# Decode block with cached attention: weights moved behind the cache rows, late weights loaded last, values in 512-column products, the output projection gathered on GpSimd

## The chip, the cores and the metric

The kernel runs on one core of a Trainium2 chip. A core has TensorE (PE, matrix products into PSUM), VectorE (DVE), ScalarE (ACT), GpSimd (POOL), a sequencer that here only issues transfers (SP), and 16 DMA engines that move data between HBM and the on-chip SBUF, a memory of 128 partitions. The engines run side by side and meet at semaphores. The metric is the device time of one execution in microseconds (us), lower is better; it is given as the median of several runs.

## The reference

One token (batch 1, sequence 1) goes through a conditioned block: modulation from `c`, layer norm, attention with 32 heads over a cache of 8192 positions with head size 192, output projection, second layer norm, and a two-layer network with a squared ReLU. All of it is float32. Cut to what matters:

```python
mod = (_silu(c) @ w_mod).reshape(c.shape[0], 6, 1, -1)      # c: 640, w_mod: 640 x 3840
sa, ca, ga, sb, cb, gb = (mod[:, 0], ..., mod[:, 5])
h = _layernorm(x) * (1 + ca) + sa
q = (h @ wq).reshape(B, Sq, 32, 192).transpose(0, 2, 1, 3)   # wq: 640 x 6144
scores = einsum("bhqd,bhkd->bhqk", q, k_cache) * 192 ** -0.5 # k_cache: 32 x 8192 x 192
o = einsum("bhqk,bhkd->bhqd", softmax(scores), v_cache)
x = x + ga * (o.reshape(B, Sq, 6144) @ wo)                   # wo: 6144 x 640
h = _layernorm(x) * (1 + cb) + sb
x = x + gb * (relu(h @ w1 + b1) ** 2 @ w2 + b2)              # w1: 640 x 1536, w2: 1536 x 640
```

The key and value caches are 201.3 MB each; wq and wo are 15.7 MB each, w_mod is 9.8 MB, w1 and w2 are 3.9 MB each. Everything is read once.

## The kernel before, in words

**Layout.** The 8192 positions of a head lie 64 to a partition, so a head's keys are a tile of 128 x 64 x 192 numbers (49,152 bytes in each partition, 6.29 MB) and its values another. Three such tiles (`slot`, line 47) fit at a time; every big load takes the next of them in turn. A load can therefore be issued only when the tile three loads earlier has been read for the last time.

**Start.** SP issues `wm0` (the columns of w_mod for sa and ca), the first pair's wq, `wm1` (the columns for ga, sb and cb) and the first head's keys. `mod` (lines 121 to 129) multiplies the modulation weights by silu(c) on TensorE; `layernorm` gives h; `query` (lines 172 to 178) makes the query of a pair of heads, already copied to all partitions.

**Loop over heads** (lines 257 to 274). Each turn issues the loads of the head's keys and values and, once for each pair of heads, a load `w` of 1.97 MB with this pair's wo and the next pair's wq (`load_w`, tiles of their own). `keys` (lines 183 to 200) works on four chunks of 16 positions: DVE multiplies the chunk by the query in place (line 190) and sums 9 to 12 of the 16 rows (line 192), ACT sums the remaining 4 to 7 (line 195). Between the chunks stand `inverse` of the head before and, in turn, `project` of the pair before (even heads) or `query` of the next pair (odd heads). `softmax` (lines 208 to 220) takes the maximum over all positions with a TensorE product, and ACT writes the exponentials 16 times side by side. `values` (lines 222 to 230) multiplies them with the values in 32 products of 384 columns (two positions each), four at a time in the four column groups of TensorE. One fp32 product is two TensorE instructions, each with a weight load.

**Project** (lines 232 to 250) scales the two heads' outputs on DVE, turns them into columns on TensorE (line 241), copies them, and multiplies them with wo into the sum `att` that stands in PSUM over the whole loop.

**End.** SP issues w1 and then `gw_t`, which holds the last columns of w_mod (gb) ahead of w2. The last pair is projected; then come x1, the second layer norm, the products with w1 (line 299), the squared ReLU, gb (`mod`, line 307), the products with w2 (line 315) and the output.

The engines' order is the order in which the program is written (`manual_schedule`); each engine works through its own instructions in that order.

Of the kernel before, what the change touches and what calls it, by code (L numbers as in the profile page):

```python
# [13 lines left out]
P = 128  # L14
D = 640
# [12 lines left out]
I = 16  # L28
NCH = NPOS // I
N_ACT = (7, 6, 6, 4)  # L30
TAIL_PARTS = 4
WO = 3 * D
WQ = KB * PW
W2_CUT = ((0, 6), (6, 5), (11, 1))
# [4 lines left out]
def block_kernel(ctx: ExitStack, tc: tile.TileContext, xc, kc, vc, wq0, wx, wo15, wm0, wm1, w1, gw2, bb, out):  # L39
# [7 lines left out]
    def slot(name):  # L47
        return strm.tile([P, NPOS * DH], F32, tag="slot", name=name, bufs=3)


# [4 lines left out]

    pick = const.tile([P, 2, 32], F32, name="pick")
    nc.vector.memset(pick[:, 0], 0.0)
    nc.vector.memset(pick[:, 1], 1.0)
    for g in range(G):
        nc.vector.memset(pick[32 * g:32 * g + 16, 0], 1.0)  # L60
        nc.vector.memset(pick[32 * g:32 * g + 16, 1], 0.0)
# [49 lines left out]


# [4 lines left out]
    nc.vector.tensor_mul(e, e, c_c)  # L117

    mods = const.tile([P, 6, DG], F32, name="mods")

    def mod(first, n, w):

        ps = psum.tile([P, 512], F32, tag="q", name=f"ps_mod{first}", bufs=2)
        for b in range(KB):
            wb = w[:, b].rearrange("p (m n) -> p m n", m=n)
            for g in range(G):
                nc.tensor.matmul(ps[32 * g:32 * (g + 1), :n * DG], e[:, b:b + 1].to_broadcast([P, 32]),  # L127
                                 wb[:, :, DG * g:DG * (g + 1)], start=(b == 0), stop=(b == KB - 1))
        nc.vector.tensor_copy(mods[:, first:first + n], ps[:, :n * DG].rearrange("p (m n) -> p m n", m=n))  # L129

    wm0_t = slot("wm0_t")
    nc.sync.dma_start(wm0_t[:, :KB * 2 * D], wm0)

    qb_t, w_t = {}, {}

    def load_w(i):

        w_t[i] = strm.tile([P, WO + WQ], F32, tag="w", name=f"w{i}", bufs=2)
        if i < 0:
            nc.sync.dma_start(w_t[i][:, WO:], wq0)  # L140
        elif i + 1 == NPAIR:
            nc.sync.dma_start(w_t[i][:, :WO], wo15)
        else:
            nc.sync.dma_start(w_t[i], wx[i])

    k_t, v_t = {}, {}

    def load(src, to, h, what):
        to[h] = slot(f"{what}{h}")
        n = TAIL_PARTS if h == H - 1 and what == "v" else 1  # L150
        w = NPOS * DH // n
        for c in range(n):
            nc.sync.dma_start(to[h][:, c * w:(c + 1) * w],
                              src[h].rearrange("(p i) d -> p (i d)", p=P)[:, c * w:(c + 1) * w])

    load_w(-1)
    wm1_t = slot("wm1_t")
    nc.sync.dma_start(wm1_t[:, :KB * 3 * D], wm1)
    load(kc, k_t, 0, "k")
    mod(0, 2, wm0_t[:, :KB * 2 * D].rearrange("p (b n) -> p b n", b=KB))  # L160
    ma = columns(mods[:, 0:2].rearrange("p m n -> p (m n)"), 2 * DG, "ma")
# [10 lines left out]
    def query(i):  # L172
        w = w_t[i - 1][:, WO:].rearrange("p (b n) -> p b n", b=KB)
        ps = psum.tile([P, 512], F32, tag="q", name=f"ps_q{i}", bufs=2)
        for b in range(KB):
            nc.tensor.matmul(ps[:, :PW], hR[:, b], w[:, b], start=(b == 0), stop=(b == KB - 1))  # L176
        qb_t[i] = work.tile([P, PW], F32, name=f"qb{i}", tag="qb")
        nc.scalar.activation(qb_t[i], ps[:, :PW], AF.Copy, scale=DH ** -0.5)

    att = psum.tile([P, 512], F32, tag="att", name="att")  # L180
    query(0)

    def keys(h, between):
# [3 lines left out]
        t = k_t.pop(h).rearrange("p (i d) -> p i d", d=DH)  # L187
        for c in range(NCH):
            pr = t[:, c * I:(c + 1) * I]
            nc.vector.tensor_mul(pr, pr, q[:, None, :].to_broadcast([P, I, DH]))  # L190
            n = I - N_ACT[c]
            nc.vector.tensor_reduce(sc[:, c * I:c * I + n], pr[:, :n], axis=AX.X, op=ALU.add)  # L192
            for i in range(n, I):
                jk = work.tile([P, DH], F32, tag="jk", name=f"jk{h}_{c}_{i}", bufs=2)
                nc.scalar.activation(jk, pr[:, i], AF.Copy, accum_out=sc[:, c * I + i:c * I + i + 1])  # L195
            if c == 0 and h:
                inverse(h - 1)
            if c == 2:
                between()
        return sc  # L200

    ri_t, ps_t, sum_t = {}, {}, {}

    def inverse(h):
        ri_t[h] = work.tile([P, 1], F32, tag="ri", name=f"ri{h}", bufs=3)
        nc.vector.reciprocal(ri_t[h], sum_t.pop(h))

    def softmax(h, sc):
# [3 lines left out]
        nc.tensor.matmul(ps[:, :P], mp.to_broadcast([P, P]), ident, start=True, stop=True)  # L212
# [3 lines left out]
        p = work.tile([P, NPOS, 16], F32, tag="p", name=f"p{h}", bufs=1)  # L216
        sp = work.tile([P, 1], F32, tag="sp", name=f"sp{h}")
        nc.scalar.activation(p, sc[:, :, None].to_broadcast([P, NPOS, 16]), AF.Exp, bias=nm, accum_out=sp)  # L218
        sum_t[h] = total(sp, f"sum{h}")
        return p  # L220

    def values(h, p):

        t = v_t.pop(h)
        ps_t[h] = psum.tile([P, 512], F32, tag="o", name=f"ps_o{h}", bufs=3)
        n = NPOS // 2
        for j in range(n):
            g = j % G
            nc.tensor.matmul(ps_t[h][32 * g:32 * (g + 1), :PW], p[:, 2 * j:2 * j + 2].rearrange("p e r -> p (e r)"),  # L229
                             t[:, PW * j:PW * (j + 1)], start=(j < G), stop=(j >= n - G))  # L230

    def project(i):
        os_ = work.tile([P, 2, PW], F32, tag="os", name=f"os{i}", bufs=1)
        for a in range(2):
            h = 2 * i + a
            nc.vector.tensor_scalar(os_[:, :, DH * a:DH * (a + 1)], ps_t.pop(h)[:, :PW].rearrange("p (e d) -> p e d", e=2),  # L236
                                    ri_t.pop(h), None, op0=ALU.mult)
        pt = psum.tile([P, 512], F32, tag="sm", name=f"ps_oT{i}", bufs=2)
        for j in range(3):
            for k in range(2):  # L240
                nc.tensor.matmul(pt[:, 32 * j:32 * (j + 1)], os_[:, k, P * j:P * (j + 1)], pick[:, k],  # L241
                                 start=(k == 0), stop=(k == 1))
        oT = work.tile([P, 96], F32, tag="oT", name=f"oT{i}")
        nc.vector.tensor_copy(oT, pt[:, :96])  # L244
# [117 lines left out]
```

## Time and profile before

| What | Value |
|---|---|
| Median of 3 runs | 1074.64 us (1073.70 to 1075.82) |
| Profiled execution, first to last instruction | 1072.6 us |
| PE / DVE / ACT / POOL busy | 431.8 / 756.2 / 320.1 / 0.7 us |
| Instructions | 8839, of them 3176 products and 3176 weight loads on PE |
| HBM read | 451.82 MB |
| Mean DMA rate | 422 GB/s |

The profile is one execution. Its page gives the busy time of each engine, a strip of 40 slices with the DMA rate, the DMA queues, the chain of waits that ended last, and groups of instructions by source line with count, busy time and the mean of one in ns. Other views give one row for a stretch of time (busy time of each engine with the number of instructions in brackets, granted TensorE clock, DMA share, GB/s), single instructions in order of time, or who waited for whom. "SPq" is SP's sequencer, where transfers are issued.

### The profile page before, as it was taken

The page shows a single profiled execution, that of the slowest core. Times are in us where ns is not written, and L with a number is a line of the kernel's source. Part 1 is how long each engine was busy: PE and PEld are TensorE (multiplying, and loading weights), DVE is VectorE, ACT ScalarE, POOL GpSimd, SP SyncE. Part 2 cuts the span into 40 slices and gives each one's busy share as a digit, 9 for nine tenths or more (in the row PEclk, how much of TensorE's full clock was granted, in tenths as well). Part 3 has the DMA queues.
Part 4 walks back from the last instruction along what each step waited for, and adds up shares of the span by engine and source line. Part 5 has one row for each costly group of instructions (what it writes and reads, how often), then busy time and mean ns, then how long its engine had stood idle before and what let it go on. Part 6 is the DMA issues. An engine that isn't in the chain of part 4 may idle for free.

```text
span 1072.6 us, 8839 instructions
## 1 busy us (share of the span) xinstructions
PE 431.8 (40%) x3176; PEld 205.0 (19%) x3176; DVE 756.2 (70%) x453; ACT 320.1 (30%) x1559; POOL 0.7 (0%) x6
## 2 busy tenths in 40 slices
PE   3243243435425353442436344242633434363246
PEld 1011121113112121211113122111312111131113
DVE  1675877858578685858868586885757778585872
ACT  1132332323233232323422233332322323232340
POOL 0000000000000000000000000000000000000000
PEclk8666566666656666575666656566665666666568
DMA  9999999999999999999999999999999999999976
GB/s 401 438 426 435 419 442 436 428 431 433 428 422 442 424 439 424 437 429 427 435 437 424 440 424 438 425 432 432 426 436 423 430 435 426 433 428 426 399 292 266
DMA packets 13299, 452.38 MB, mean 422 GB/s; under 512 B 1732, under 2 KB 1736, under 8 KB 2120
## 3 DMA queue, kind: packets, MB, share of 16 engines
q1 hardware_dynamic: 12968, 451.81, 98.1%
q8 instruction: 25, 0.41, 0.2%
q14 instruction: 18, 0.15, 0.0%
q10 hardware_dynamic: 288, 0.01, 0.0%
HBM read 451.82 MB, written 0.00 MB: 421 GB/s over the span
## 4 chain that ended last, share of the span: by engine, by line
DMA 41%; DVE 38%; PE 18%; ACT 2%; issue 1%; SPq 0%; DVEq 0%; ACTq 0%
DMA k<-in_kc 41%; DVE k L190 21%; DVE sc L192 14%; PE ps_o L229 11%; PE ps_oT L241 4%; ACT p L218 2%; PE ps_mx L212 1%; PE ps_sum L88 1%; DVE os L236 1%; DVE nm L214 0%; PE ps_f L299 0%; DVE oT L244 0%; DVE mp L210 0%; PE ps_y L315 0%; ACT L218 0%
## 5 line engine op out<-in xcount | busy, mean ns | idle before, releaser
L190 DVE TENSOR_TENSOR k<-k,qb 128x3072 f32<-128x3072 f32 x128 | 428.5, 3348 | 192.9 <-DMA k<-in_kc 192.9
L195 ACT ACTIVATE jk<-k 128x192 f32<-128x192 f32 x736 | 256.5, 349 | 614.5 <-DVE k L190 614.5
L192 DVE TENSOR_REDUCE sc<-k 128x10 f32<-128x1920 f32 (+2 forms) x128 | 282.0, 2203 | 4.4
L229 PE MATMUL ps_o<-v,p 128*32 128x384 f32 x2048 | 240.0, 638 | 2.2 <-DMA v<-in_vc 2.2
L241 PE MATMUL ps_oT<-pick,os 128*128 128x32 f32 x192 | 43.2, 395 | 266.1 <-DVE os L236 266.1
L212 PE MATMUL ps_mx<-ident,mp 128*128 128x128 f32 x64 | 25.4, 501 | 285.6 <-DVE mp L210 285.6
L195 ACT ACTIVATION_READ_ACCUMULATOR jk<-k 128x1 f32 x736 | 137.3, 186 | 0.0
L229 PEld LDWEIGHTS ps_o<-v,p 128*32 128x32 f32 x2048 | 75.6, 140 | 144.9 <-issue 142.2
L241 PEld LDWEIGHTS ps_oT<-pick,os 128*128 128x128 f32 x192 | 41.0, 321 | 277.3 <-DVE os L236 276.6
L212 PEld LDWEIGHTS ps_mx<-ident,mp 128*128 128x128 f32 x64 | 16.1, 311 | 304.8 <-DVE mp L210 273.7
L218 ACT ACTIVATE p<-sc,nm 128x1024 f32<-128x1024 f32 x32 | 36.7, 1147 | 80.9 <-DVE nm L214 80.8
L176 PE MATMUL ps_q<-w,hR 128*128 128x384 f32 x150 | 52.4, 496 | 0.1
L88 PE MATMUL ps_sum<-sp,ones 128*128 128x1 f32 x64 | 18.8, 363 | 56.5 <-ACT p L218 56.5
L176 PEld LDWEIGHTS ps_q<-w,hR 128*128 128x128 f32 x150 | 27.3, 190 | 25.5 <-issue 8.8
L248 PE MATMUL att<-w,oT 128*32 128x160 f32 x384 | 28.5, 464 | 5.6 <-DVE oT L244 5.6
L244 DVE COPY oT<-ps_oT 128x96 f32<-128x96 f32 x16 | 4.1, 258 | 36.2 <-PE ps_oT L241 36.2
L214 DVE TENSOR_REDUCE nm<-ps_mx 128x1 f32<-128x128 f32 x32 | 9.3, 292 | 28.5 <-PE ps_mx L212 28.5
L88 PEld LDWEIGHTS ps_sum<-sp,ones 128*128 128x128 f32 x64 | 16.1, 313 | 65.9 <-ACT p L218 65.9
L236 DVE TENSOR_SCALAR os<-ps_o,ri 128x384 f32<-128x384 f32 x32 | 18.2, 607 | 7.3 <-PE ps_o L229 7.3
L248 PEld LDWEIGHTS att<-w,oT 128*32 128x32 f32 x384 | 15.6, 162 | 11.9 <-DVE oT L244 7.7
L127 PE MATMUL ps_mod<-wm_t,silu 128*32 128x320 f32 (+1 forms) x80 | 9.3, 626 | 12.5 <-DVE silu L117 12.5
L129 DVE COPY mods<-ps_mod 128x320 f32<-128x320 f32 (+2 forms) x3 | 1.4, 479 | 15.4 <-PE ps_mod L127 15.4
(68 smaller groups left out, 76.5 us busy)
## 6 DMA issues: line engine op xcount, KB each, us to landing
k<-in_kc SPq DMA_DIRECT2D x32, 6144.0 KB, 29.0
v<-in_vc SPq DMA_DIRECT2D x31, 6144.0 KB, 25.7
w<-in_wx SPq DMA_DIRECT2D x15, 1920.0 KB, 34.3
v<-in_vc SPq DMA_DIRECT2D x4, 1536.0 KB, 15.8
wm_t<-in_wm SPq DMA_DIRECT2D x1, 4800.0 KB
w_t<-in_w SPq DMA_DIRECT2D x1, 3840.0 KB, 12.6
gw_t<-in_gw SPq DMA_DIRECT2D x1, 3520.0 KB, 20.5
wm_t<-in_wm SPq DMA_DIRECT2D x1, 3200.0 KB, 10.7
```

The source lines that it names most:

```text
L88: nc.tensor.matmul(ps[:, :1], ones, src, start=True, stop=True)
L127: nc.tensor.matmul(ps[32 * g:32 * (g + 1), :n * DG], e[:, b:b + 1].to_broadcast([P, 32]), wb[:, :, DG * g:DG * (g + 1)], start=(b == 0), s ...
L176: nc.tensor.matmul(ps[:, :PW], hR[:, b], w[:, b], start=(b == 0), stop=(b == KB - 1))
L190: nc.vector.tensor_mul(pr, pr, q[:, None, :].to_broadcast([P, I, DH]))
L192: nc.vector.tensor_reduce(sc[:, c * I:c * I + n], pr[:, :n], axis=AX.X, op=ALU.add)
L195: nc.scalar.activation(jk, pr[:, i], AF.Copy, accum_out=sc[:, c * I + i:c * I + i + 1])
L212: nc.tensor.matmul(ps[:, :P], mp.to_broadcast([P, P]), ident, start=True, stop=True)
L218: nc.scalar.activation(p, sc[:, :, None].to_broadcast([P, NPOS, 16]), AF.Exp, bias=nm, accum_out=sp)
L229: nc.tensor.matmul(ps_t[h][32 * g:32 * (g + 1), :PW], p[:, 2 * j:2 * j + 2].rearrange("p e r -> p (e r)"), t[:, PW * j:PW * (j + 1)], star ...
L236: nc.vector.tensor_scalar(os_[:, :, DH * a:DH * (a + 1)], ps_t.pop(h)[:, :PW].rearrange("p (e d) -> p e d", e=2), ri_t.pop(h), None, op0=A ...
L241: nc.tensor.matmul(pt[:, 32 * j:32 * (j + 1)], os_[:, k, P * j:P * (j + 1)], pick[:, k], start=(k == 0), stop=(k == 1))
L248: nc.tensor.matmul(att[32 * g:32 * (g + 1), :DG], oT[:, 32 * j:32 * (j + 1)], w[:, j, DG * g:DG * (g + 1)], start=(i == 0 and j == 0), sto ...
```

## The change

- **Loads.** The pair's weights no longer have loads and tiles of their own. A slot is 14,208 numbers wide: 12,288 of keys and 1,920 of weights. The keys of the even heads 0 to 28 carry the next pair's wq, those of the odd heads 3 to 31 the wo of the pair before; the last values carry the last wo. The first load holds sa's and ca's weights, the first wq and all small vectors. The last keys are loaded in two halves, the last values in one piece.
- **Late weights.** The weights of ga, sb, cb and gb are no longer loaded at the start; after the last values come `wm1` (all four), `w1`, and `w2`. The issue of `w2` stands in the program behind the last projection.
- **Start.** sa and ca: DVE weighs and adds the weights (`weigh`), TensorE sums over partitions with ones.
- **Keys.** One multiplication of all 64 positions. Then GpSimd adds the two halves of 28 rows (`N_FOLD`), ACT sums 4 rows, DVE sums 32 whole rows, does what stands in `between`, and sums the 28 folded rows (96 numbers each). The last head does this in two halves.
- **Softmax.** The exponentials are written 8 times instead of 16; the sums over partitions are taken once for a pair.
- **Values.** The columns of the value cache are split into 128 and 64; 16 products take four positions of the first part, 8 products eight of the second: 24 products of 512 columns. Each group of rows holds the wanted numbers in one of its blocks only, so DVE then multiplies by a mask and adds the blocks (`own`).
- **Projection.** `turn` makes one column of the pair's outputs on TensorE and ACT copies it. GpSimd multiplies wo by this column and adds the three parts into `acc` (`gather`), at the odd heads from 3 on, ahead of the fold in GpSimd's order. Only the last pair goes through TensorE, together with `acc`.
- **End.** `gather` also makes gb's weighted sum on GpSimd. Line 303's and 304's operations on f become one.

```diff
-I = 16
-N_ACT = (7, 6, 6, 4)
+ROW = KV + WO
+DA = 128
+DB = DH - DA
+REP = 8
+N_FOLD = 28
+N_ACT = 4
...
+    def load_k(h):
+        k_t[h] = slot(f"k{h}")
+        n = ROW if h not in (1, H - 2) else KV
+        cuts = (0, KV // 2, n) if h == H - 1 else (0, n)
+        for a, b in zip(cuts, cuts[1:]):
+            nc.sync.dma_start(k_t[h][:, a:b], kx[h, :, a:b])
+
+    def load_v(h):
+        v_t[h] = slot(f"v{h}")
+        n = ROW if h == H - 1 else KV
+        nc.sync.dma_start(v_t[h][:, :n], vx[h, :, :n])
...
+    def weigh(to, w):
+        nc.vector.tensor_scalar(to, w[:, 0], e[:, 0:1], None, op0=ALU.mult)
+        for b in range(1, KB):
+            nc.vector.scalar_tensor_tensor(to, w[:, b], e[:, b:b + 1], to, op0=ALU.mult, op1=ALU.add)
+
+    def gather(to, w, s):
+        nc.gpsimd.tensor_mul(w, w, s[:, :, None].to_broadcast(list(w.shape)))
+        for j in range(w.shape[1]):
+            nc.gpsimd.tensor_add(to, to, w[:, j])
...
     def keys(h, between):
...
-        for c in range(NCH):
-            pr = t[:, c * I:(c + 1) * I]
-            nc.vector.tensor_mul(pr, pr, q[:, None, :].to_broadcast([P, I, DH]))
...
+        parts = 2 if h == H - 1 else 1
+        n = NPOS // parts
+        for c in range(parts):
+            pr = t[:, c * n:(c + 1) * n]
+            s = sc[:, c * n:(c + 1) * n]
+            nc.vector.tensor_mul(pr, pr, q[:, None, :].to_broadcast([P, n, DH]))
+            nf, na = N_FOLD // parts, N_ACT // parts
+            a, b = n - nf - na, n - na
+            nc.gpsimd.tensor_add(pr[:, a:b, :DH // 2], pr[:, a:b, :DH // 2], pr[:, a:b, DH // 2:])
+            for i in range(b, n):
                 jk = work.tile([P, DH], F32, tag="jk", name=f"jk{h}_{c}_{i}", bufs=2)
-                nc.scalar.activation(jk, pr[:, i], AF.Copy, accum_out=sc[:, c * I + i:c * I + i + 1])
+                nc.scalar.activation(jk, pr[:, i], AF.Copy, accum_out=s[:, i:i + 1])
+            nc.vector.tensor_reduce(s[:, :a], pr[:, :a], axis=AX.X, op=ALU.add)
+            if c == 0:
                 between()
+            nc.vector.tensor_reduce(s[:, a:b], pr[:, a:b, :DH // 2], axis=AX.X, op=ALU.add)
         return sc
...
     def values(h, p):
...
+        o_t[h] = psum.tile([P, 1024], F32, tag="o", name=f"ps_o{h}", bufs=2)
+        na, nb = NPOS // 4, NPOS // 8
+        for c in range(na):
+            g = c % G
+            nc.tensor.matmul(o_t[h][32 * g:32 * (g + 1), :512], p[:, 4 * c:4 * c + 4].rearrange("p e r -> p (e r)"),
+                             t[:, 512 * c:512 * (c + 1)], start=(c < G), stop=(c >= na - G))
+        for c in range(nb):
+            g = c % G
+            nc.tensor.matmul(o_t[h][32 * g:32 * (g + 1), 512:],
+                             p[:, 8 * c:8 * c + 8, ::2].rearrange("p e r -> p (e r)"),
+                             t[:, 512 * (na + c):512 * (na + c + 1)], start=(c < G), stop=(c >= nb - G))
+
+    def own(h):
+        i, a = h // 2, h % 2
...
+        if a:
+            ri_t[i] = work.tile([P, 2], F32, tag="ri", name=f"ri{i}")
+            nc.vector.reciprocal(ri_t[i], sum_t.pop(i))
+            nc.vector.tensor_scalar(os_t[i][:, :DH], os_t[i][:, :DH], ri_t[i][:, 0:1], None, op0=ALU.mult)
+        scale = ri_t.pop(i)[:, 1:2] if a else 1.0
+        m = big(f"own{h}", 1024)
+        nc.vector.scalar_tensor_tensor(m, o_t.pop(h), scale, mask, op0=ALU.mult, op1=ALU.mult)
+        nc.vector.tensor_reduce(to[:, :DA], m[:, :512].rearrange("p (j d) -> p d j", d=DA), axis=AX.X, op=ALU.add)
+        nc.vector.tensor_reduce(to[:, DA:], m[:, 512:].rearrange("p (j d) -> p d j", d=DB), axis=AX.X, op=ALU.add)
...
     for h in range(H):
         i = h // 2
...
+        if h:
+            load_k(h)
+        load_v(h)
+        if h % 2 and i:
+            gather(acc, k_t[h][:, KV:ROW].rearrange("p (j n) -> p j n", j=3), oT_t.pop(i - 1))
...
         def between():
+            if h % 2 == 0 and i + 1 < NPAIR:
+                query(i + 1, k_t[h][:, KV:ROW])
+            if h:
+                own(h - 1)
             if h % 2 == 0 and h:
-                project(i - 1)
-            elif h % 2 and i + 1 < NPAIR:
-                query(i + 1)
+                oT_t[i - 1] = turn(i - 1)
...
+    wm1_t = slot("wm1_t")
+    nb = KB // 2 + 1
...
     w1_t = slot("w1_t")
...
+    mod(0, nb)
+    own(H - 1)
+    oT = turn(NPAIR - 1)
+    att = psum.tile([P, 512], F32, tag="q", name="att", bufs=2)
+    for g in range(G):
+        nc.tensor.matmul(att[32 * g:32 * (g + 1), :DG], ones[:, :32], acc[:, DG * g:DG * (g + 1)], start=True, stop=False)
...
+    mod(nb, KB)
+    w2_t = slot("w2_t")
     for b0, n in W2_CUT:
...
+        nc.sync.dma_start(w2_t[:, b0 * D:(b0 + n) * D], w2[:, b0 * D:(b0 + n) * D])
...
+    gather(gb_w, wm1_t[:, :, 3], e)
```

More of the change, by code (lines that the diff above doesn't have):

```diff
@@ L38, in block_kernel @@
 @with_exitstack
[L39 removed]
+def block_kernel(ctx: ExitStack, tc: tile.TileContext, first, kx, vx, wm1, w1, w2, out):
     nc = tc.nc
@@ L117, in block_kernel @@
     nc.vector.tensor_mul(e, e, c_c)
[L119 to L161, printed above, removed]
+    nc.vector.tensor_copy(x_c, vec[:, KB:2 * KB])
+    nc.vector.tensor_copy(bbc, vec[:, 2 * KB:])
+    ma_w = big("ma_w", 2 * D)
+    weigh(ma_w, first_t[:, :WM].rearrange("p (b n) -> p b n", b=KB))
+    ps = psum.tile([P, 512], F32, tag="q", name="ps_ma", bufs=2)
+    for g in range(G):
+        nc.tensor.matmul(ps[32 * g:32 * (g + 1), :2 * DG], ones[:, :32],
+                         ma_w.rearrange("p (m n) -> p m n", m=2)[:, :, DG * g:DG * (g + 1)], start=True, stop=True)
+    ma_s = const.tile([P, 2 * DG], F32, name="ma_s")
+    nc.vector.tensor_copy(ma_s, ps[:, :2 * DG])
+    ma = columns(ma_s, 2 * DG, "ma")
     ca1 = const.tile([P, KB], F32, name="ca1")
@@ L220, in softmax @@
+        if h % 2:
+            sum_t[i] = total(sp_t.pop(i), f"sum{i}")
         return p
     def values(h, p):
[L224 to L237, printed above, removed]
+        t = v_t[h]
```

193 lines of the change are left out of this document (107 added, 86 removed).

## The prediction

> **What bounds the kernel now.** I read the page's totals, strip and queues first, then the chain, then the waits, then stretches of the trace.
>
> ```profile
> span 1072.6 us, 8839 instructions
> PE 431.8 (40%) x3176; PEld 205.0 (19%) x3176; DVE 756.2 (70%) x453; ACT 320.1 (30%) x1559; POOL 0.7 (0%) x6
> GB/s 401 438 426 435 419 442 436 428 431 433 428 422 442 424 439 424 437 429 427 435 437 424 440 424 438 425 432 432 426 436 423 430 435 426 433 428 426 399 292 266
> q1 hardware_dynamic: 12968, 451.81, 98.1%
> q8 instruction: 25, 0.41, 0.2%
> DMA 41%; DVE 38%; PE 18%; ACT 2%; issue 1%; SPq 0%; DVEq 0%; ACTq 0%
> ```
>
> No engine is busy over 70%; the data queue is, at 98.1%. The chain runs through keys, softmax and values to the next load of keys, but a chain only says which wait came last. The waits and one long stretch decide:
>
> ```profile
> DVE k L190 <- DMA k<-in_kc: 192.9, 31, 10.8
> ...
> SPq L153 <- DVE sc L192: 633.9, 31, 28.9
> SPq L153 <- PE ps_o L229: 316.3, 30, 12.0
> ```
> ```profile
> 104.05:989.40 885.35, 359.70 (x2548) 170.67 (x2548) 649.43 (x350) 274.90 (x1358) 0.00 (x0) 0.63 1.00 431
> ```
> ```profile
> 1032.50:1039.50 7.00, 0.34 (x1) 0.34 (x2) 6.47 (x4) 2.01 (x12) 0.00 (x0) 0.50 0.02 9
> ```
> ```profile
> 1058.00:1072.60 14.60, 9.63 (x176) 5.84 (x176) 3.98 (x11) 0.00 (x0) 0.00 (x0) 0.85 0.33 135
> ```
>
> DVE waits 6 us a head for keys: it has slack. From the landing of head 2's keys to that of head 30's the DMA share is 1.00; 14 pairs take 885.35 us, 63.24 a pair, and a pair reads 4 x 6.29 + 1.97 = 27.13 MB, so 429 GB/s. The middle is bound by the transfers. Only the end is not: 7 us with an empty queue before w1 is issued, and the last 14.6 us at a third.
>
> **The steady part.** The bytes stay the same, so the time stays as long as each load is issued before the queue runs dry. All heads now read 7.27 + 6.29 = 13.56 MB, 31.6 us. The values of head h+1 take the slot of the keys of head h, so `keys` must be done before the next keys have landed, 31.6 us after its own. How much earlier: the first late load shows it.
>
> ```profile
> 1038.85 0.33 SPq L278 DMA_DIRECT2D w_t<-in_w  x1
> ```
> ```profile
> 1039.50:1040.00 0.50, 0.46 (x2) 0.16 (x1) 0.01 (x1) 0.00 (x0) 0.00 (x0) 0.50 2.25 614
> ```
> ```profile
> w_t<-in_w SPq DMA_DIRECT2D x1, 3840.0 KB, 12.6
> ```
>
> Issue to first data is about 1 us; of the 12.6 us 9.2 are 3.93 MB at 429, so up to 2.4 lie behind the data. I take 1.9 in all (bounds 1.0 and 3.4): the deadline is 29.7 us after landing. Now the work of a head:
>
> ```profile
> L190 DVE TENSOR_TENSOR k<-k,qb 128x3072 f32<-128x3072 f32 x128 | 428.5, 3348 | 192.9 <-DMA k<-in_kc 192.9
> ...
> L192 DVE TENSOR_REDUCE sc<-k 128x10 f32<-128x1920 f32 x64 | 137.8, 2153 | 2.2
> ...
> L192 DVE TENSOR_REDUCE sc<-k 128x12 f32<-128x2304 f32 x32 | 81.7, 2553 | 1.1
> ...
> L218 ACT ACTIVATE p<-sc,nm 128x1024 f32<-128x1024 f32 x32 | 36.7, 1147 | 80.9 <-DVE nm L214 80.8
> ...
> L127 PE MATMUL ps_mod<-wm_t,silu 128*32 128x480 f32 x40 | 4.2, 568 | 0.0
> ...
> L302 DVE TENSOR_TENSOR f<-ps_f,bbt 128x384 f32<-128x384 f32 x1 | 0.6, 557 | 4.9 <-PE ps_f L299 4.9
> ...
> L303 DVE TENSOR_SCALAR f<-f 128x384 f32<-128x384 f32 x1 | 0.4, 359 | 0.0
> ...
> masks.py:199 POOL TENSOR_SCALAR_AFFINE_SELECT ident<-ident 128x128 f32<-128x128 f32 x1 | 0.3, 293 | 0.1
> ...
> L355 POOL MEMSET const-float32-0.0<- 128x1 f32 x1 | 0.1, 99 | 0.2 <-issue 0.2
> ```
>
> Between the shapes DVE pays 1.04 ns an element and 0.16 us an instruction. So: multiplication of 12,288 elements 12.9; 32 rows (6,144) 6.55; `own` 1,024 elements 1.23 and two sums of 512 1.39, together 2.6, with reciprocal and scaling 3.1 at even heads; folded rows (2,688) 2.95. That is 25.5 at even and 25.0 at odd heads, under the deadline of 29.7. `own`'s sums read with a stride, which no row shows: at double price they add 1.1 us, still hidden; below that nothing is to be had. ACT loses 19 of 23 sums and half the exponentials (1.15 to about 0.6): ACT waits for DVE most of the time, worth nothing here. The values keep their columns (32 x 384 = 24 x 512), so I keep their 8 us (by instructions 6); they release the next keys' slot about 11 us after `keys` (softmax 2.9, values 8), at 37, needed at 44. If that cover went, each us late would cost 16 us in all.
>
> GpSimd is the open price: no row has two operands. With one it pays (293 - 99) / 128 = 1.5 ns an element; two taken one after the other would be 3.0. I take 2.27, in the middle, and 0.1 us each: the fold (2,688) 6.2 us (4.2 to 8.2), `gather` (1,920 and three times 640) 9.1 (6.2 to 12.0). At even heads the fold lies beside DVE's 6.55 + 3.1. At odd heads `gather` starts when the keys land and lies beside the 12.9 us multiplication; the fold then starts in time. Cost 0 if the two engines don't hold each other up; if they do, see the first rival.
> The Trainium skill has a price for it (GPSIMD Engine Reference, section 3.1): 4497 ns for an addition of 2,048 elements, an estimate of 2.2 ns an element, close to my middle; the sum by it would be 0.2 us lower.
>
> Instructions: PE's 6,352 fit 0.41 MB in 25 packets (65 bytes each), so q8 is TensorE's own code. A third less is 0.14 MB. Spread over 16 engines that saves 0.3 us, all on one engine (429 / 16 = 26.8 GB/s) 5.1. I take 2.
>
> **The start.** The first load is 4.27 MB, wm1 (4.92) is gone from ahead of the keys.
>
> ```profile
> 28.11 0.49 ACT L178 ACTIVATE qb<-ps_q 128x384 f32<-128x384 f32 x1 [7.60 <-PE ps_q L176]
> ...
> 39.89 3.36 DVE L190 TENSOR_TENSOR k<-k,qb 128x3072 f32<-128x3072 f32 x1 [4.51 <-DMA k<-in_kc]
> ```
>
> `weigh` costs DVE five times 1,280 elements, 7.4 us, where TensorE took 5: the query is ready near 31, when 11.5 MB have landed too. Keys 0 start 8 us sooner, with the queue full either way: 0. The masks are made before the first load lands.
>
> **The end.** It begins with head 30's keys, for the transfers set that moment. Behind it lie 29.4 MB before (keys 31, values 30 and 31, wo, w1, gb with w2) and 35.3 after (the same with wq's and wo's place taken by 6.55 MB of late weights): 5.9 MB, 13.7 us, earlier. With 2 us for instructions: 989.4 - 15.7 = 973.7.
>
> ```profile
> 989.40 3.36 DVE L190 TENSOR_TENSOR k<-k,qb 128x3072 f32<-128x3072 f32 x1 [10.61 <-DMA k<-in_kc]
> ...
> 1036.23 2.55 DVE L192 TENSOR_REDUCE sc<-k 128x12 f32<-128x2304 f32 x1
> ...
> 1042.19 8.06 PE L229 MATMUL ps_o<-v,p 128*32 128x384 f32 x64
> ...
> 1051.00 1.08 PE L241 MATMUL ps_oT<-pick,os 128*128 128x32 f32 x8 [0.19 <-DVE os L236]
> ...
> 1053.52 0.33 DVE L292 TENSOR_TENSOR x<-att,mods 128x160 f32<-128x160 f32 x1 [1.15 <-PE att L248]
> ```
> ```profile
> 1065.69 3.47 PE L315 MATMUL ps_y<-gw_t,fT 128*32 128x160 f32 x96 [1.02 <-DVE fT L74]
> ```
>
> Before, it takes 64.1 us from there to x1 (1053.5). After, counted from the landing: `keys` of head 30 25.7, its maximum 1.5: 27.2. Head 31, first half: multiplication 6.55 (33.8), 16 rows 3.35, `own` 2.6 (39.8). But its fold stands on GpSimd behind `gather`, which waits for the second half of these keys (31.6): 9.1, fold 3.15, so 43.9. DVE waits 4.1, then 1.55 (45.4). Second half 6.55 + 3.35 + 1.55: 56.9. Softmax 2.9 (before 3.4 from 1038.8 to 1042.2, less half the exponentials), values 8.06: 67.8. `own` 2.6 in place of a 0.6 us scaling: 70.4. From the turn to x1 2.5 as before, four products of `acc` 0.35, the rest of `mod` (16 of 40 products of 4.2) 1.7, a copy 0.3: 75.3. So x1 starts at 1049.0, 4.5 sooner. Behind it one operation on f is gone (0.36): -0.4. The transfers keep pace: values 31 land at 1022, wm1 at 1038, w1 at 1047 (the layer norm's end is near 1054). w2 is issued behind `att`, at 1047, waits about 1 and takes 9.2: it lands near 1058, its products start at 1061. SP has only the output behind it. gb's `gather` on GpSimd (3,200 and five of 640, 15 us from 1038) is done at 1053.
>
> **Sum**: 1072.6 - 15.7 + 11.2 - 0.4 = 1067.7 for the profiled execution. The median of the runs shown is 2.0 above the span (1074.64 to 1072.6), so 1069.7; I say 1069.5. By GpSimd's ends the 4.1 us of waiting are 0 or 8: 1065.5 to 1073.6.
>
> **Rivals.**
> (1) DVE's multiplication and GpSimd's `gather` exclude each other: 0.38. Both read two SBUF operands; before, GpSimd does nothing in the loop, so nothing in the trace speaks against it. Then at odd heads the chain is 12.9, `gather` 9.1, fold 6.2, folded rows 2.95 = 31.2, 1.5 past the deadline; 14 such heads 21 us, with 3 more at the end (`gather` starts at 33.8, x1's adds): 1094. It decides from 2.04 ns an element ((29.7 - 12.9 - 2.95 - 0.5) / 6,528): at 1.5 it costs only the 3 less what GpSimd's speed gives, near 1069; at 3.0 it is 36.1, 6.4 late, near 1160.
> The Trainium skill (SBUF — State Buffer, section "Who interferes with whom") states just this: a VectorE instruction with two SBUF inputs and a GpSimd instruction that reads SBUF hold one read port by turns, for whole instructions. No run shown tests it. By that page's rule and the other page's 2.2 ns the sum would be about 1080, slower.
> (2) TensorE's code loading sits on one DMA engine and holds the rest up: 0.08. Then the full 5.1 us count: 1066.5. For it speaks one row: near the end one engine of 16 still works when the others are done.
>
> ```profile
> 1034.50:1035.00 0.50, 0.00 (x0) 0.00 (x0) 0.50 (x1) 0.00 (x0) 0.00 (x0) 0.50 0.06 25
> ```
>
> (3) The end gains nothing: 0.08. `own` at the double price (+1.1 twice), longer handovers to GpSimd and the values with a colder clock (0.50 where the values of head 31 start, 10 us in place of 8) add 5: 1074.5, no change.
>
> **How the numbers follow.** My forecast has 0.46, its own range 1065 to 1074. What a measurement can tell is about 0.2%, 2.1 us: faster is under 1072.5, slower over 1076.8. Faster: 0.44 of the forecast, the 0.08 of (2), 0.02 of (1): 0.54. Same: 0.02 + 0.02 + 0.04 = 0.08. Slower: 0.36 of (1), 0.02 of (3): 0.38. The range 1062 to 1097 leaves out about 0.15 of (1) and 0.03 below.
>
> **What would show it.** DMA share 1.00 and 31.6 us a head in the middle: the steady part is right; gaps of the queue after odd heads, with DVE waiting for GpSimd ahead of the folded rows: (1). DVE's 12,288-element multiplication at 12.9 us at odd and even heads alike: no hold-up on DVE. GpSimd's 2,688-element addition near 6.2 us. Head 30's keys landing near 974, x1 near 1049. It is wrong if GpSimd is slower than 3 ns an element, or the long rows of the keys load at less than 429 GB/s.

## The result and the profile after

The changed kernel takes 1098.72 us (1097.29 to 1100.62, 4 runs) where the one before, run again beside it, takes 1075.03 (1073.70 to 1075.82, 4 runs): 1.0221 times as long, 95% interval 1.0206 to 1.0236. It is 2.2% slower; the forecast was 1069.5, 0.5% faster, with a range to 1097. What happened is the first rival, put at 1094.

The page of the changed kernel: totals, the strip of DMA rates, the data queue, and the chain by engine.

```profile
span 1095.5 us, 5419 instructions
...
PE 368.5 (34%) x2088; PEld 132.9 (12%) x2088; DVE 873.5 (80%) x341; ACT 89.0 (8%) x361; POOL 500.6 (46%) x107
...
GB/s 411 429 418 436 431 400 425 409 430 429 398 433 407 437 438 397 429 398 433 386 438 427 398 430 403 435 415 433 429 398 448 388 436 413 421 417 358 448 411 190
...
q1 hardware_dynamic: 10520, 451.83, 96.5%
...
DMA 35%; POOL 35%; PE 14%; DVE 12%; issue 3%; ACT 1%; POOLq 0%; DVEq 0%; ACTq 0%; SPq 0%
```

A third of TensorE's instructions is gone as announced. But GpSimd, busy for 0.7 us before, now has a third of the chain, and slices near 400 GB/s alternate with full ones. The groups by shape (count, busy time, mean in ns, idle time before) and DVE's waits say where:

```profile
L210 DVE TENSOR_TENSOR k<-k,qb 128x12288 f32<-128x12288 f32 x31 | 404.6, 13050 | 102.0 <-DMA k<-in_kx 98.1 <-ACT qb L192 3.4
L151 POOL TENSOR_TENSOR k<-k,oT 128x1920 f32<-128x1920 f32 x15 | 216.6, 14437 | 218.7 <-DMA k<-in_kx 203.8 <-issue 14.9
...
L213 POOL TENSOR_TENSOR k<-k 128x2688 f32<-128x2688 f32 x31 | 181.9, 5866 | 336.3 <-DVE k L210 316.2 <-issue 20.1
L220 DVE TENSOR_REDUCE sc<-k 128x28 f32<-128x2688 f32 x31 | 91.4, 2949 | 55.2 <-POOL k L213 55.2
L153 POOL TENSOR_TENSOR acc<-acc,k 128x640 f32<-128x640 f32 x45 | 81.7, 1815 | 3.5
```
```profile
DVE k L210 <- DMA k<-in_kx: 98.1, 20, 7.0
DVE sc L220 <- POOL k L213: 60.0, 15, 4.8
```

`gather`'s product of 1,920 elements (line 151) takes 14.4 us, while GpSimd does 2,688 elements of the fold in 5.9. One odd head in order of time (start, duration):

```profile
447.88 12.96 DVE L210 TENSOR_TENSOR k<-k,qb 128x12288 f32<-128x12288 f32 x1 [6.45 <-DMA k<-in_kx]
460.87 6.55 DVE L217 TENSOR_REDUCE sc<-k 128x32 f32<-128x6144 f32 x1
...
474.77 2.95 DVE L220 TENSOR_REDUCE sc<-k 128x28 f32<-128x2688 f32 x1 [4.19 <-POOL k L213]
```
```profile
447.94 16.14 POOL L151 TENSOR_TENSOR k<-k,oT 128x1920 f32<-128x1920 f32 x1 [14.76 <-DMA k<-in_kx]
464.16 4.77 POOL L153 TENSOR_TENSOR acc<-acc,k 128x640 f32<-128x640 f32 x3
468.88 5.86 POOL L213 TENSOR_TENSOR k<-k 128x2688 f32<-128x2688 f32 x1
```
```profile
477.79 0.33 SPq L99 DMA_DIRECT2D v<-in_vx  x1
```

The keys land and release both engines. DVE multiplies until 460.84. GpSimd's product starts 0.06 us later and ends 3.2 us after DVE's. The additions and the fold follow, DVE waits 4.19 us for the fold, and the next values' load is issued 29.9 us after the keys' landing. Two stretches of this kernel (length, busy times, granted clock, DMA share, GB/s): the moment of that issue, and heads 3 to 29.

```profile
476.50:478.50 2.00, 0.31 (x1) 0.18 (x1) 1.44 (x2) 0.00 (x0) 0.00 (x0) 0.50 0.00 0
```
```profile
124.02:966.85 842.83, 286.26 (x1528) 100.59 (x1524) 685.66 (x234) 66.92 (x286) 421.11 (x78) 0.63 0.98 419
```

The queue stands empty for 2 us before these values. Thirteen pairs take 842.83 us, 64.83 a pair. The kernel before takes 63.26 between the same heads:

```profile
132.75:955.12 822.37, 334.23 (x2368) 158.91 (x2368) 603.03 (x325) 255.27 (x1261) 0.00 (x0) 0.63 1.00 431
```

The end, DVE's instructions of the changed kernel:

```profile
997.86 12.95 DVE L210 TENSOR_TENSOR k<-k,qb 128x12288 f32<-128x12288 f32 x1
...
1042.91 1.55 DVE L220 TENSOR_REDUCE sc<-k 128x14 f32<-128x1344 f32 x1 [4.85 <-POOL k L213]
...
1072.62 0.32 DVE L347 TENSOR_TENSOR x<-att,mods 128x160 f32<-128x160 f32 x1
1072.98 2.19 DVE L348 TENSOR_TENSOR x<-x,x_t 128x160 f32<-128x160 f32 x1
...
1076.74 1.65 DVE L133 SCALAR_TENSOR_TENSOR ln_sq<-ln_xm 128x160 f32<-128x160 f32 x1
```

So the 22.9 us between the two profiled executions (1095.5 and 1072.6) have three parts. Head 30's multiplication starts 8.5 us later (997.86 in place of 989.40). From there to x1 it takes 74.8 us in place of 64.1 (+10.6), and from x1 to the end 22.9 in place of 19.1 (+3.8).

### The profile page after: what moved, and what is told of

Its sections match the earlier page's. It is cut to its first block, busy times and chain, and to the rows that moved or that the text cites. A ratio compares the mean times of both kernels' runs of the same rounds, so it can differ in the third digit from the quotient of the medians.

```text
span 1095.5 us, 5419 instructions
## 1 busy us (share of the span) xinstructions
PE 368.5 (34%) x2088; PEld 132.9 (12%) x2088; DVE 873.5 (80%) x341; ACT 89.0 (8%) x361; POOL 500.6 (46%) x107
## 4 chain that ended last, share of the span: by engine, by line
DMA 35%; POOL 35%; PE 14%; DVE 12%; issue 3%; ACT 1%; POOLq 0%; DVEq 0%; ACTq 0%; SPq 0%
DMA k<-in_kx 34%; POOL k L151 20%; PE ps_o L248 8%; POOL k L213 8%; POOL acc L153 7%; DVE sc L220 5%; DVE k L210 3%; PE ps_o L252 2%; DVE sc L217 2%; DMA first_t<-in_first 1%; PE ps_sum L119 1%; PE ps_mx L227 1%; DVE ma_w L147 1%; ACT p L235 1%; PE ps_f L357 1%
## 5 line engine op out<-in xcount | busy, mean ns | idle before, releaser
L210 DVE TENSOR_TENSOR k<-k,qb 128x12288 f32<-128x12288 f32 (+1 forms) x33 | 417.7, 12656 | 102.0 <-DMA k<-in_kx 98.1
L213 POOL TENSOR_TENSOR k<-k 128x2688 f32<-128x2688 f32 (+1 forms) x33 | 187.9, 5694 | 344.4 <-DVE k L210 324.4
L151 POOL TENSOR_TENSOR k<-k,oT 128x1920 f32<-128x1920 f32 x15 | 216.6, 14437 | 218.7 <-DMA k<-in_kx 203.8
L217 DVE TENSOR_REDUCE sc<-k 128x32 f32<-128x6144 f32 (+1 forms) x33 | 209.8, 6359 | 1.1
L248 PE MATMUL ps_o<-v,p 128*32 128x512 f32 x1024 | 188.8, 904 | 21.9 <-ACT p L235 21.9
L220 DVE TENSOR_REDUCE sc<-k 128x28 f32<-128x2688 f32 (+1 forms) x33 | 94.5, 2864 | 60.0 <-POOL k L213 60.0
L216 ACT ACTIVATE jk<-k 128x192 f32<-128x192 f32 x128 | 44.8, 351 | 499.5 <-DVE k L210 480.8
L153 POOL TENSOR_TENSOR acc<-acc,k 128x640 f32<-128x640 f32 x45 | 81.7, 1815 | 3.5
L252 PE MATMUL ps_o<-v,p 128*32 128x512 f32 x512 | 60.5, 592 | 0.0
L190 PE MATMUL ps_q<-k,hR 128*128 128x384 f32 x150 | 52.3, 496 | 0.0
L269 DVE TENSOR_REDUCE os<-own 128x128 f32<-128x512 f32 x32 | 33.7, 1053 | 1.1
L216 ACT ACTIVATION_READ_ACCUMULATOR jk<-k 128x1 f32 x128 | 23.8, 186 | 0.0
```

The source lines that it names most:

```text
L151: nc.gpsimd.tensor_mul(w, w, s[:, :, None].to_broadcast(list(w.shape)))
L153: nc.gpsimd.tensor_add(to, to, w[:, j])
L213: nc.gpsimd.tensor_add(pr[:, a:b, :DH // 2], pr[:, a:b, :DH // 2], pr[:, a:b, DH // 2:])
L216: nc.scalar.activation(jk, pr[:, i], AF.Copy, accum_out=s[:, i:i + 1])
L217: nc.vector.tensor_reduce(s[:, :a], pr[:, :a], axis=AX.X, op=ALU.add)
L220: nc.vector.tensor_reduce(s[:, a:b], pr[:, a:b, :DH // 2], axis=AX.X, op=ALU.add)
```

## The experiments

**Theory A**: GpSimd's product and DVE's multiplication exclude each other; the fold comes late, the keys' slot is released late, the queue runs dry. **Theory B**: no wait matters; long rows or the new order of loads are slower. **Theory C**: GpSimd's product with a broadcast factor is slow by itself. "A pair" is the time from the start of head 3's multiplication to that of head 29's, over 13; it comes from the one profiled execution of each kernel, the median from all its runs.

| Kernel | Head 3, head 29 | A pair | Median us | Ratio to before (95%) |
|---|---|---|---|---|
| before | 132.75, 955.12 | 63.26 | 1075.03 | |
| changed | 124.02, 966.85 | 64.83 | 1098.72 | 1.0221 (1.0206 to 1.0236) |
| sum left out | 123.95, 938.01 | 62.62 | 1063.66 | 0.9896 (0.9881 to 0.9910) |
| sum on DVE | 124.39, 952.97 | 63.74 | 1078.84 | 1.0050 (1.0031 to 1.0070) |
| sum behind the fold | 123.89, 948.73 | 63.45 | 1072.05 | 0.9979 (0.9965 to 0.9994) |
| 16 rows folded | 124.01, 948.72 | 63.44 | 1080.60 | 1.0051 (1.0035 to 1.0067) |
| left out, more code | 125.34, 940.61 | 62.71 | 1064.31 | 0.9898 (0.9882 to 0.9915) |
| wo behind the values | 122.36, 951.75 | 63.80 | 1081.10 | 1.0060 (1.0045 to 1.0075) |
| the same, gb on TensorE | 121.89, 947.73 | 63.53 | 1076.11 | 1.0011 (0.9999 to 1.0023) |
| the same, 12 rows on ACT | 121.26, 942.62 | 63.18 | 1064.82 | 0.9913 (0.9895 to 0.9932) |
| four multiplications | 123.72, 988.74 | 66.54 | 1122.01 | 1.0438 (1.0423 to 1.0454) |
| query in PSUM | 124.76, 940.05 | 62.71 | 1067.18 | 0.9933 (0.9916 to 0.9950) |
| query in PSUM, shorter sums | 123.50, 938.36 | 62.68 | 1060.07 | 0.9861 (0.9846 to 0.9876) |
| sum behind the fold, shorter sums | 123.30, 938.93 | 62.74 | 1057.04 | 0.9837 (0.9822 to 0.9851) |
| the same, weights loaded apart | 120.75, 937.87 | 62.86 | 1057.56 | 0.9843 (0.9826 to 0.9859) |

**1. The sum over wo left out.**

```diff
-        if h % 2 and i:
-            gather(acc, k_t[h][:, KV:ROW].rearrange("p (j n) -> p j n", j=3), oT_t.pop(i - 1))
```

> The weighted sum of wo on GpSimd in the loop is left out (15 of 16 pairs' projection is missing from the output); all else stays, the loads too. Theory A (GpSimd's product waits for DVE's multiplication, so the fold and the release of the keys' slot come late and the queue runs dry): the wait of DVE for the fold is gone at odd heads, a pair goes from 64.9 us back to 63.2 or a little less, 14 pairs save 23 us, the last head another 5: median 1071. Theory B (no wait matters; rows of 56,832 bytes, or the changed order of loads, move fewer bytes a second): a pair stays at 64.9 us, only the 5 us of the last head go: 1094.

The kernel takes 35 us less than the changed one, 7 under what was expected, and the loop runs faster than before the change, not only as fast. So neither the rows' length nor the order of the loads is a cost:

```profile
123.95:938.01 814.06, 280.51 (x1512) 99.59 (x1508) 681.38 (x234) 66.92 (x286) 152.70 (x26) 0.64 1.00 433
```

The same loads run at 433 GB/s with a DMA share of 1.00. Theory B falls.

**2. The sum on DVE.**

```diff
+            if h % 2 and i:
+                for j in range(3):
+                    nc.vector.scalar_tensor_tensor(acc, w[:, j], s[:, j:j + 1], acc, op0=ALU.mult, op1=ALU.add)
             if h:
                 own(h - 1)
```

> The same sum over wo on DVE: three operations of 640 elements (0.83 us each by DVE's slope) at the odd heads, between the whole rows and the head before's own blocks; GpSimd keeps only the fold. Theory A: keys end at 25.9 + 2.5 = 28.4 us after landing at odd heads, in place of 29.9; a pair is 63.2 to 63.6 us; the last head loses its 4.9 us wait and pays 2.5: median 1074 to 1079. Theory B: 64.9 us a pair, 1096.

The median is where it was expected, a pair slightly above (63.74; 63.2 to 63.6 was expected). An odd head, from the start of the multiplication to the issue of the next values' load:

```profile
443.63 12.96 DVE L210 TENSOR_TENSOR k<-k,qb 128x12288 f32<-128x12288 f32 x1 [6.36 <-DMA k<-in_kx]
```
```profile
471.86 0.33 SPq L99 DMA_DIRECT2D v<-in_vx  x1
```

With the issue 28.2 us after the landing, a pair still loses 1.1 us against the first experiment, so 29.7 is no safe deadline. The queue shows why in part: in the 1.5 us around this issue at the odd heads (0.8 us before to 0.7 after) it moves 236 GB/s in the mean, next to nothing in the changed kernel.

**3. The sum behind the fold.** Only the order on GpSimd changes.

```diff
             nc.gpsimd.tensor_add(pr[:, a:b, :DH // 2], pr[:, a:b, :DH // 2], pr[:, a:b, DH // 2:])
+            if c == parts - 1:
+                late()      # gather of the pair before, at odd heads from 3 on
```

> The sum over wo stays on GpSimd but stands behind the fold in GpSimd's order (in the last head behind the second fold). Nothing is removed. Theory A: the product takes about 3.4 us, since DVE only sums rows then; it ends 12.96 + 5.9 + 3.4 + 4.8 = 27.1 us after landing; keys end at 25.9; a pair is 63.2 us; median 1072. Theory B: 64.9 us a pair, 1094. Theory C (the product with a broadcast factor takes 16 us on GpSimd by itself, whatever DVE does): the slot is released 40 us after landing, some 10 us late at each odd head: over 1200.

GpSimd in an odd head of this kernel:

```profile
516.06 5.87 POOL L213 TENSOR_TENSOR k<-k 128x2688 f32<-128x2688 f32 x1 [26.02 <-DVE k L210]
521.89 3.39 POOL L151 TENSOR_TENSOR k<-k,oT 128x1920 f32<-128x1920 f32 x1
525.36 4.76 POOL L153 TENSOR_TENSOR acc<-acc,k 128x640 f32<-128x640 f32 x3
```

The same product takes 3.39 us beside DVE's sums over rows, 16.14 beside its multiplication. Theory C falls, and with the order alone changed the kernel is 0.2% faster than before. A pair (63.45) still loses 0.8 us against the first experiment, although the queue around the issue, now 27.2 us after landing, shows no gap (469 GB/s in the mean, 449 in the first experiment).

**4. Fewer rows folded.**

```diff
-N_FOLD = 28
+N_FOLD = 16
```

> 16 folded rows in place of 28; the sum over wo stays where the change put it. DVE pays 12 more whole rows (2.4 us) less 12 half rows (1.2). Theory A: the product over wo still takes 16.1 us, but the fold only 3.5, so it ends at 24.7 us after landing and DVE doesn't wait for it; keys end near 27.2 at odd and 27.5 at even heads; if the limit is near 28.3 a pair is 63.2 us and the median 1077; DVE's own lateness would show here. Theory B: 64.9 us a pair, 1098.

DVE no longer waits for the fold in the loop, and most of the loss there is gone, though the product still waits its 13 us. So that wait by itself costs little; what fits is the release, now near 27 us after landing at all heads. A pair is at 63.44, not at 63.2, and the median is 3.6 us over the expectation.

**5. More of TensorE's code.**

```diff
         values(h, softmax(h, sc))
+        for j in range(17):
+            nc.tensor.matmul(more_t[h][:32, 256 + j:257 + j], ones[:, :32], ones[:, :1], start=True, stop=True)
```

> As the kernel without the sum over wo (15 pairs' projection left out), plus 17 idle one-column products behind each head's values, 2,176 more TensorE instructions: about as many as the change removed. They run while TensorE has nothing to do. Rival 2 of the prediction (TensorE's code sits on one DMA engine and holds the data up): 0.14 MB on one engine, up to 0.3 us a pair, median about 1068 in place of 1063.7. If the code is spread over the engines or hidden: within 0.5 us of 1063.7.

```profile
PE 394.2 (37%) x3176; PEld 171.7 (16%) x3176; DVE 868.8 (82%) x341; ACT 89.0 (8%) x361; POOL 203.1 (19%) x47
```

TensorE has as many instructions as before the change, and there is no measurable difference to the first experiment (0.9898 to 0.9896, intervals nearly the same). Fewer instructions are not what makes the loop faster.

**6. wo behind the values' rows.**

```diff
+    def with_wo(h):
+        return h in (H - 2, H - 1) or h % 2 and 3 <= h < H - 1
...
-        n = ROW if h not in (1, H - 2) else KV
+        n = ROW if h % 2 == 0 and h < H - 2 else KV
...
-        n = ROW if h == H - 1 else KV
+        n = ROW if with_wo(h) else KV
```

> Nothing left out. As the kernel with the sum behind the fold, but wo lies behind the values' rows of the odd heads (and of head 30) in place of the keys', so that the sum no longer keeps the keys' slot, only the values', which has more time. Theory A in its finer form (each us of later release of the keys' slot costs, already at 27 us after landing): release at 26 us, a pair at 62.6 to 62.9 us in place of 63.4, median 1065. If the 0.8 us a pair between the kernel without the sum and the kernel with it behind the fold come from GpSimd's work itself: 63.4 us, median 1071.

This is a miss: the kernel is 9 us slower than with wo behind the keys. The odd heads' keys no longer keep their slot long, but the landings are uneven now. 7.27 + 7.27 MB lie between an odd head's keys and the next, 6.29 + 6.29 between an even head's and the next. Even heads, whose keys end 26.2 us after landing, have 29.0 us to the next landing in place of 31.3. So the remedy seems to have brought the same lateness at the other heads; run 8 bears on that.

**7. gb on TensorE** (and all of 6).

```diff
-    gb_w = big("gb_w", D)
-    nc.gpsimd.memset(gb_w, 0.0)
-    gather(gb_w, wm1_t[:, :, 3], e)
...
+    for b in range(KB):
+        for g in range(G):
+            nc.tensor.matmul(ps_g[32 * g:32 * (g + 1), :DG], e[:, b:b + 1].to_broadcast([P, 32]),
+                             wm1_t[:, b, 3, DG * g:DG * (g + 1)], start=(b == 0), stop=(b == KB - 1))
```

> As the one before, and gb's weighted sum is done by TensorE (20 products of 160 columns) in place of GpSimd, so that GpSimd does nothing beside the second layer norm. If the 2.2 and 1.65 us of two DVE operations there (0.33 each alone) are waits for GpSimd, 3.2 us go from the end: median 1062 if the one before is at 1065. If these are slow for another reason, no difference.

The two DVE operations of the second layer norm, with GpSimd at work beside them (kernel 6) and without (kernel 7):

```profile
1056.63 2.19 DVE L355 TENSOR_TENSOR x<-x,x_t 128x160 f32<-128x160 f32 x1
...
1060.39 1.66 DVE L136 SCALAR_TENSOR_TENSOR ln_sq<-ln_xm 128x160 f32<-128x160 f32 x1
```
```profile
1051.64 0.33 DVE L352 TENSOR_TENSOR x<-x,x_t 128x160 f32<-128x160 f32 x1
...
1053.33 0.33 DVE L136 SCALAR_TENSOR_TENSOR ln_sq<-ln_xm 128x160 f32<-128x160 f32 x1
```

Here DVE is the one that waits. From x1 to the end it is 19.6 us in place of 23.4. This kernel's times spread over 6 us (1072.89 to 1078.90, 10 runs), and the profile is of the fastest of them; why they spread stays open.

**8. More rows on ACT** (and all of 7).

```diff
-N_FOLD = 28
-N_ACT = 4
+N_FOLD = 24
+N_ACT = 12
```

> As the one before, with ACT summing 12 rows and GpSimd folding 24 (4 and 28 before): DVE sums 28 whole rows and 24 halves, 1.2 us less a head. If a pair is at the limit of the transfers (62.6 us), only the last two heads' 2.4 us show: median 1059 to 1060. If earlier release still buys time in the middle, more.

The median is 11 us better, where 2.4 was expected at least. The two profiled executions differ by 8.0: 5.6 up to head 30's multiplication and 2.3 in the last two heads. The rest lies in the spread of kernel 7. So a release 1.2 us earlier still buys time where the landings are uneven.

**9. Four multiplications in place of one** (from the changed kernel).

```diff
-            nc.vector.tensor_mul(pr, pr, q[:, None, :].to_broadcast([P, n, DH]))
+            for m in range(0, n, 16):
+                nc.vector.tensor_mul(pr[:, m:m + 16], pr[:, m:m + 16], q[:, None, :].to_broadcast([P, 16, DH]))
```

> The changed kernel, with DVE's multiplication of the keys cut into four of 3,072 elements (as before the change); the sum over wo stays ahead of the fold. If the read port is held for one instruction and then handed over: GpSimd's product takes at most 3.35 + 3.4 us, one of DVE's four is about 3.4 us longer, others 1.6 longer for the three additions; DVE's multiplying then takes 13.4 + 8.2 = 21.6 us, the fold is in time, keys end near 34 us after landing: worse, 68 us a pair, median above 1130. If DVE's instructions keep the port in a row: the product takes about 16.8 us as before and the pair 65 to 65.5 us, median 1100 to 1106.

An odd head, DVE and GpSimd:

```profile
457.13 19.02 DVE L211 TENSOR_TENSOR k<-k,qb 128x3072 f32<-128x3072 f32 x4 [6.92 <-DMA k<-in_kx]
```
```profile
457.20 6.54 POOL L151 TENSOR_TENSOR k<-k,oT 128x1920 f32<-128x1920 f32 x1 [15.10 <-DMA k<-in_kx]
463.81 13.74 POOL L153 TENSOR_TENSOR acc<-acc,k 128x640 f32<-128x640 f32 x3
```

The two engines take turns, an instruction each: the product ends 3.35 + 3.2 us after the landing, and the four multiplications take 19.0 in place of 13.4. The expectation of 21.6 was 2.6 too long, in the main because the third addition comes behind the last multiplication. The median, 1122, lies between the two expected (above 1130 with the handover, 1100 to 1106 without); the instructions' order decides for the handover.

**10. The query in PSUM** (from the changed kernel). The multiplication keeps its place, its length and its neighbour; its second operand comes from PSUM, and ACT's copy of the query to SBUF is gone.

```diff
-    nc.vector.tensor_copy(hR, h1[:, :, None].to_broadcast([P, KB, P]))
+    nc.vector.tensor_scalar(hR, h1[:, :, None].to_broadcast([P, KB, P]), DH ** -0.5, None, op0=ALU.mult)
...
-        qb_t[i] = work.tile([P, PW], F32, name=f"qb{i}", tag="qb")
-        nc.scalar.activation(qb_t[i], ps[:, :PW], AF.Copy, scale=DH ** -0.5)
+        qb_t[i] = ps[:, :PW]
```

> The changed kernel, but the query stays in PSUM, so that DVE's multiplication has one SBUF operand (the scale of the scores goes to the copy of h); the sum over wo stays where the change put it, beside that multiplication. If GpSimd's product waits because DVE reads two operands from SBUF: it now takes 3.4 us, DVE's multiplication stays at 12.9 to 13.0, the fold starts with its end, a pair is 62.6 to 62.9 us, median 1067 to 1069. If any work of DVE on the same tile holds GpSimd up: 16 us and 65 us a pair as in the changed kernel.

```profile
438.13 12.96 DVE L209 TENSOR_TENSOR k<-k,ps_q 128x12288 f32<-128x12288 f32 x1 [4.16 <-DMA k<-in_kx]
438.19 3.39 POOL L151 TENSOR_TENSOR k<-k,oT 128x1920 f32<-128x1920 f32 x1 [12.47 <-DMA k<-in_kx]
441.66 4.78 POOL L153 TENSOR_TENSOR acc<-acc,k 128x640 f32<-128x640 f32 x3
...
451.16 5.87 POOL L212 TENSOR_TENSOR k<-k 128x2688 f32<-128x2688 f32 x1 [4.72 <-DVE k L209]
```

They run side by side, and neither is longer than alone: the product takes 3.39 us, the multiplication 12.96. 31.5 us are won, as expected. This settles theory A and names its cause: it is DVE's second SBUF operand that holds GpSimd up.

**11 and 12. Versions that beat both.** Both have gb on TensorE, 16 rows on ACT and 20 folded; 11 has the query in PSUM, 12 the query in SBUF and the sum behind the fold.

> Query in PSUM, gb on TensorE, 16 rows on ACT and 20 folded. Keys end near 24.5 us after landing at all heads; a pair at 62.6 us; the end 3.2 us shorter by gb and some 5 by the shorter sums of the last two heads: median 1056 to 1060, faster than both kernels.

> As the one before, but with the query in SBUF and the sum over wo behind the fold. The slot of the odd heads' keys is released at 12.96 + 4.3 + 8.2 = 25.4 us after landing, as early as DVE's end in the kernel without the sum: a pair at 62.6 to 62.8 us, median 1057 to 1061. If the release of the keys' slot isn't what the 0.8 us a pair of the sum behind the fold were, 63.4 us a pair and 1068.

```profile
span 1054.5 us, 6271 instructions
...
GB/s 404 434 438 427 438 437 425 443 429 433 434 434 425 443 425 440 433 434 424 444 429 440 433 429 429 442 431 437 431 425 431 437 428 441 427 429 409 431 430 323
```
```profile
123.30:938.93 815.63, 280.48 (x1516) 99.49 (x1512) 640.21 (x234) 174.70 (x910) 214.03 (x78) 0.64 1.00 433
```

Number 12 is the fastest, 1.6% faster than before: the loop stays at 433 GB/s, and the last slice but one is still at 430 (292 before). GpSimd does the same sum as in run 3, and a pair is back at 62.7 with the release at 25.6 us, so that sum by itself isn't what costs the 0.8 us of run 3. It beats 11 at the end, where the last head's sum doesn't stand ahead of its first fold: DVE waits 3.49 us for that fold in 11, not at all in 12.

**13. The weights loaded apart** (from 12).

```diff
-        cuts = (0, KV // 2, n) if h == H - 1 else (0, n)
+        cuts = (0, KV // 2, n) if h == H - 1 else (0, KV, n) if n > KV else (0, n)
```

> As the kernel with the sum behind the fold, gb on TensorE and 16 rows on ACT, but each load of keys with weights is made in two: 49,152 bytes of keys a row, then 7,680 bytes of weights. If separate loads with short rows are what the kernel before loses 0.55 us a pair by: a pair goes from 62.74 to 63.2 us or more, median 1064 to 1068. If not: 62.7 us and 1057, and the difference to the kernel before stays open.

There is no difference (1057.56 to 1057.04; 0.9843 to 0.9837 of the kernel before). Why the loop before the change takes 63.26 us a pair and not 62.7 stays open: neither TensorE's code (5) nor separate loads with short rows (13) explain it.

## Why the prediction was wrong, point by point

- **What bounds the kernel**: right; the transfers bound the middle. But a DMA share of 1.00, taken for a full queue, is too blunt: it stands at 1.00 from 62.6 to 63.7 us a pair (runs 1 and 2), and only the rate shows the loss (433 GB/s in run 1, 428 in run 3, 426 in run 2, 419 with a share of 0.98 in the changed kernel).
- **The step that failed** is in the steady part: "At odd heads `gather` starts when the keys land and lies beside the 12.9 us multiplication ... Cost 0". Both start together, as said, but the product doesn't run: 16.14 us in place of 3.39, so DVE waits 4.19 us for the fold and a pair takes 64.83 us in place of the 62.6 without the sum. I gave this the chance of a rival, 0.38, because no row of the trace before showed GpSimd at work beside DVE.
 The Trainium skill (SBUF — State Buffer, section "Who interferes with whom") states this hold-up for two SBUF operands, and its section "SBUF: two separate sides" that it lasts for whole instructions. Run 10 agrees with the first (3.39 us with one operand in PSUM, 16.14 with two in SBUF), run 9 with the second (the product waits 3.35 us, one multiplication). The forecast should have gone by it.
- **The price of that rival** came near (1.5 us a pair forecast, 1.57 measured against the kernel before; total 1094 to 1098.7), but by luck. Its chain was too long: 31.2 us where the keys end 29.9 after landing, since `gather` and the fold were put at 15.3 and take 14.0. By its own deadline of 29.7 that would have cost 0.2 us a pair. Against the loop without the sum the loss is 2.2.
- **The deadline** of 29.7 us (bounds 28.2 to 30.6) was too late, and it isn't a sharp limit. With 31.3 us from landing to landing and keys released at 25.0 to 26.2 us (runs 1, 10 and 12) a pair takes 62.6 to 62.7; at 27.2 at the odd heads (run 3) 63.45, at 28.2 (run 2) 63.74, at 29.9 (changed) 64.83. Why a release at 27.2 costs, where no gap of the queue shows, stays open.
- **GpSimd's prices**: right within 6% for the fold (5.87 us for the 6.2 put down). The product was sized 4.5 and takes 3.39 alone; an addition of 640 takes 1.54, as put down. One working in the text doesn't come out: at 2.2 ns an element and its own 0.1 us an instruction, the sum is 0.4 us lower and not 0.2, and rival 1 gives about 1086 and not 1080.
- **DVE's prices**: right for the multiplication (12.96), the whole rows (6.55) and the folded rows (2.95). `own` takes 3.3 us in place of 2.6: its sums with a stride are 1.03 each, between the 0.69 taken and the 1.23 of the upper bound.
- **The start**: head 0's multiplication begins 6.5 us sooner (33.44 to 39.89), 8 forecast; either way the text priced it at 0.
- **Instructions** (2 us, rival 2's 5): nothing (run 5).
- **The end**, from head 30's keys to x1: 75.3 forecast, 74.8 measured. Errors cancel in it: the last head's wait for its fold is 4.85 (4.1 forecast, 6.3 with rival 1) and `own` is longer, the values take 6.9 in place of 8.06. It began 24.2 us later than forecast (997.86 to 973.7): 22 of that are 14 pairs at 1.57, and DVE started behind the keys' landing.
- **x1 to the end**: forecast 0.4 shorter, measured 3.8 longer; 3.2 of it are the same hold-up, by gb's sum (2.19 and 1.65 in place of 0.33 each). The text had that in rival 1 as "x1's adds", at about 1 us. It also had gb's sum run from 1038 to 1053; it starts at 1069.5 only, because `gb_w` takes the one buffer that the last `own` uses (`big`, line 56 of the changed kernel):

```profile
1068.88 0.63 POOL L341 MEMSET gb_w<- 128x640 f32 x1 [14.85 <-DVE os L270]
```

- **The range** took in rival 1 at 1094 and ended at 1097; with the deadline's earlier bound it would have had to reach past 1110.

## What to carry to other kernels

Work that moves to GpSimd doesn't run beside DVE's just because the engines differ. Look at whether the DVE instruction that is to cover it reads two operands from SBUF; if so, give it one from PSUM, or put GpSimd's work beside row sums. Where three slots feed a full DMA queue, a later release costs before it shows as an empty queue: here, by one profile of each kernel, 1 us of later release cost an estimated 0.3 to 0.7 us a pair from 26 us on, 5 us before the next landing. The order of two pieces of work on an engine that isn't the bottleneck (the sum ahead of the fold) can be the whole loss: changing it won 27 us.

## What the hardware showed that was not expected

- At 14 odd heads one load releases both engines, and DVE gets ahead in 13 of them: 13 products of 16.14 us and two of 3.4 make the 216.6. At head 3 GpSimd was ahead; DVE's multiplication took 15.85 us in place of 12.96, and then the additions waited instead (17.36 in place of 4.77). At head 31 the weights come with the second half of the keys, and the product runs beside row sums in 3.39.

```profile
124.02 15.85 DVE L210 TENSOR_TENSOR k<-k,qb 128x12288 f32<-128x12288 f32 x1 [4.47 <-DMA k<-in_kx]
```
```profile
127.14 17.36 POOL L153 TENSOR_TENSOR acc<-acc,k 128x640 f32<-128x640 f32 x3
```

- The wait shows as busy time of GpSimd: 16.14 us of "work" for 1,920 elements. The sign is the mean of one instruction against another of its kind, not the idle column.
- A product with a broadcast factor takes GpSimd 1.77 ns an element (3.39 us for 1,920), an addition of two full operands 2.2 (5.87 for 2,688). Whether the broadcast or the multiplication makes the difference, no run separates.
